# A second weight piece split ahead of the expert stage, its banks ordered by release, and new ranks for an instruction planner

## The chip, the core and the metric

The kernel runs on one core of a Trainium2 chip. The metric is the device time of one execution in microseconds, taken as the median of several runs. TensorE multiplies matrices into eight PSUM banks; VectorE (DVE), ScalarE (ACT) and GpSimd (POOL) do the work between the products; SyncE (SP) issues most of the loads and stores.

## The reference

Three layers follow each other, on 4 sequences of 576 tokens with 8 heads of 64:

```python
scores = scale * q @ k.T ; causal mask ; a = softmax(scores) ; local = a @ v
q_p = where(q > 0, q, exp(q) - 1) + 1
mem_out = (q_p @ M_prev) / (q_p @ z_prev + 1e-6)
x = sigmoid(beta) * mem_out + (1 - sigmoid(beta)) * local      # tokens 2304 x 512
logits = x @ w_gate ; e = argmax(logits) ; gate = softmax(logits)[e]
y[e tokens] = gate * (relu(x @ w1[e]) @ w2[e])                 # 8 experts, 512 -> 1024 -> 512
h = y @ w_in ; g = where(h > 0, h, exp(min(h, 0)) - 1)
out = g @ w_out                                                # 512 -> 2048 -> 512
```

## The kernel before

**Three stages.** Attention handles 16 pairs of heads (`pair(p)`, four pairs to a sequence). The expert stage (`moe`) handles tiles of 128 tokens of one expert (`mtile(t)`, NTM = 23 of them). The last layer is `moe2`. Each stage is a `phase`: its operations are declared with a cost and a priority, and `Plan.order` on the host lists them in time. At each step it takes the engine that can start earliest, and among the operations that could start within `slack` of that moment the one of lowest priority number. The instructions are issued engine by engine in the order of that list. So a priority decides only between operations that the plan holds for ready at nearly the same time, and a cost that is told wrongly moves instructions on every engine. The dictionary `KNOBS` holds the priorities (`off` per step of a pair; `m_x`, `m_1`, `m_h`, `m_fl` per kind of step of a tile), the engines that may take a step (`es`, `xe`, `wh`), and the slack of attention (`sa`) and of the expert stage (`sm`).

**A pair.** TensorE turns k and q (L92), makes five blocks of scores (L645, L649, L656), turns the exponentials back (L92), and multiplies them with v (L748). It then multiplies the result by the identity and the gate's weights (L538, `rw`), and VectorE reads that out, scaled (L777), and adds the memory part (L789; on GpSimd except in the last pair).

**The gate and routing.** After each sequence `gate_plan` picks the experts and writes a table (L824 to L903); after three of them `routing(early)` names the first NE = 4 tiles, whose weights are then loaded (`tile_weights`, L1120) and whose tokens are gathered. The fourth gate and the second routing (L936 to L1033) run inside the expert stage.

**A tile.** Products are made in three parts: high half by high half, low by high, high by low. So each of eight weight pieces of 128x1024 needs a cast to its high half (L1162 on DVE, L1159 on ACT in tile 0) and a subtraction for its low half (L1165, DVE only). Piece n = 2k + q lies in raw bank k. For tiles after the first the two steps stand behind a flag that skips them when the expert is the one of the tile before (`wsplit`, `fh` and `fl`, L1264 and L1269; two pieces to a step; the plan counts `m_if` for each). A tile's first product (L1288) uses pieces 0 to 3, its second (L1331) pieces 4 to 7; between them stand the ReLU (L1298), the transposes (L1313) and the split of the hidden values (L1159, L1165).

**The seam.** `first_parts` prepares tile 0 inside attention: it turns the gathered tokens (L1145), splits them (`x0`), and splits the pieces in `c.wq`, which is piece 0 alone, with the low priority `first`. These buffers lie in the pool `ep`, which outlives attention's pool `ap`. All other buffers of the expert stage lie in `mp`, which takes the place of `ap`. The expert stage has eight PSUM banks: four for the first product (`c.rg`), three for transposes, gate and routing (`c.rt`), one for the second product (`c.ry`). Attention uses the same memory as four tiles of two banks (`c.rx`).

Of the kernel before, what the change touches and what calls it, by code (L numbers as in the profile page):

```python
# [39 lines left out]
NS = 8  # L40
assert NE <= -(-((B - 1) * S - E * (P - 1)) // P)
# [53 lines left out]
class Plan:  # L95
# [140 lines left out]
    "xe": ("ACT", "DVE"), "he": ("ACT",), "re": [("ACT",), ("ACT", "DVE")], "m_ld": 3500.0, "m_x": -2208.9, "m_1": -1447.9, "m_h": -4434.5, "m_lag": 0.0,  # L236
    "m_if": 700.0, "m_fl": -3000.0, "m_wl": 300.0, "wa": 0, "wa0": 10022.449169040721, "wa1": 23927.854833523612, "wt": 1, "wp": 16, "wj": 2000.0,
# [3 lines left out]
    "nv": 2, "na": 2, "na4": 2, "nx": 2, "nls": 2, "wide": 1, "de": ("DVE", "POOL"), "busy": [0, 0, 0], "early": 120578.4, "late": 500, "mld": -2631.6,  # L241
    "gate": 345828.7, "warm": [52, 0.0, 200.0], "qe": ("DVE",),
    "off": {"tk": 898454.0, "tq": 882278.5, "hk": -760325.6, "hq": -759364.9, "px": 735151.8, "phi": 1087364.4, "S3": -529669.6, "S4": -1296033.8, "S2": -790035.1, "S1": -972813.3, "S0": -1302605.5, "min3": -50550.3, "min4": -410935.5, "min2": 719181.7, "min1": -45115.7, "min0": 332677.3, "exp3": 329358.7, "exp4": 631684.7, "exp2": -50550.0, "exp1": 518666.4, "exp0": 344677.0, "T3": 859665.0, "T4": 626578.9, "T2": 622423.5, "T1": 518666.8, "T0": 516520.2, "Te3": -47668.1, "Te4": 807182.8, "Te2": -1296012.9, "Te1": -509705.8, "Te0": -561958.2, "fin": -50955.8, "mm": 807201.2, "md": -1303158.8, "ms": 238704.4, "avA": -328031.8, "avB": -684654.8, "ave": -328185.5, "rw": -1410391.2, "ls": -829501.3, "add": -8135.8},
    "es": {"x": ("ACT",), "T0": ("ACT",), "T3": ("ACT",), "k": ("ACT", "DVE"), "T1": ("ACT", "DVE"), "T4": ("ACT", "DVE"), "q": ("ACT", "DVE"), "T2": ("ACT", "DVE")},
    "wait": 25, "first": 1087370.1, "stick": 1227967.1,
# [222 lines left out]
def cv(n):  # L468
    return 70 + 1.04 * n
# [705 lines left out]
def moe(tc, c, w1, w2, tiles):  # L1175
# [30 lines left out]
    def mtile(t):  # L1206
        pr = 1000.0 * t
        rw = t % 2 if t < NTM else 1
# [20 lines left out]
        if t:  # L1229
            pl.op("PE", 436, f, r=[sg], w=[wx], prio=pr + K["m_x"])  # L1230
        else:
            xh.index, xl.index = r_xh.free.pop(0)[1], r_xl.free.pop(0)[1]
        for _ in range(t > 0):
            split(c, lambda: wx.t, lambda: xh.t.rearrange("p c n -> p (c n)"), lambda: xl.t.rearrange("p c n -> p (c n)"), 512,
                  [wx], xh, xl, pr + K["m_x"], True, K["xe"], ("DVE",))

        flags = {}
        for e, eng in (("ACT", mybir.EngineType.Activation), ("DVE", mybir.EngineType.DVE)) if t else ():
            def mk(e, eng):
# [5 lines left out]
                pl.op(e, 450, f, r=[("sw", part)], w=[("flag", e, t)], prio=pr + K["m_fl"])  # L1245
            mk(e, eng)

        def wsplit(k, pr):
# [4 lines left out]
            if not t:  # L1253
                for q in range(2):
# [3 lines left out]
                    split(c, lambda q=q: src(q), lambda n=n: whi[n], lambda n=n: wlo[n], 1024, [("raw", rw, k)], keys[0][q], keys[1][q], pr, False, K["wh"][n], K["wl"][n])  # L1258
# [11 lines left out]
            pl.op("ACT", K["m_if"], fh, r=[("flag", "ACT", t), ("raw", rw, k)], w=keys[0], prio=pr)  # L1270
            pl.op("DVE", K["m_if"], fl, r=[("flag", "DVE", t), ("raw", rw, k)] + keys[0], w=keys[1], prio=pr)
# [4 lines left out]
        for cc in range(4):  # L1276
            def mk(cc):
                p1 = pr + K["m_1"] + 10 * cc
# [16 lines left out]
        for hf in range(2):  # L1295
            def mk(hf):
# [3 lines left out]
                def fv():  # L1300
# [3 lines left out]
                      prio=pr + K["m_h"])  # L1304
            mk(hf)
        hs = []
        for k in range(2):
            def mk(k):
                wt, hh, hl = Slot(rt), Slot(r_hh), Slot(r_hl)

                def f():
                    for j in range(4):
                        nc.tensor.transpose(wt.t[:, j * P:(j + 1) * P], sh.t[:, (4 * k + j) * P:(4 * k + j + 1) * P], c.ident)  # L1313
                pl.op("PE", 436, f, r=[(sh, k)], w=[wt], prio=pr + K["m_h"])
                split(c, lambda: wt.t, lambda: hh.t.rearrange("p c n -> p (c n)"), lambda: hl.t.rearrange("p c n -> p (c n)"), 512,
                      [wt], hh, hl, pr + K["m_h"], True, K["he"], ("DVE",))
# [4 lines left out]
        for q in range(4):  # L1321
            def mk(q):
# [11 lines left out]
                for jj in range(2):  # L1334
                    pl.op("PE", 3 * 216, mm(jj), r=[hh, hl, *wk], w=[y], prio=pr + 10 * q)
# [12 lines left out]
        pl.op(("ACT", "DVE"), (ca(512), cv(512)), (fa, fv), r=[y, sg], w=[sy], prio=pr + 500)  # L1348
# [248 lines left out]
def kernel(ctx, tc, q, k, v, M_prev, z_prev, beta, w_gate, w1, w2, w_in, w_out, out):  # L1597
# [43 lines left out]
    with ExitStack() as s1:  # L1641
# [3 lines left out]
        c.wq = [[ep.tile([P, 1024], F32R, name=f"wq{n}{i}") for i in range(2)] for n in range(1)]  # L1645
# [24 lines left out]
        with ExitStack() as s2:  # L1670
# [5 lines left out]
            banks, _ = psum(s2, "pm", 8)  # L1676
            c.rg, c.rt, c.ry = Ring("g", banks[:4]), Ring("t", banks[4:7]), Ring("y", banks[7:])
            
            def build():
# [3 lines left out]
                routing(tc, c, c.rt, False, c.K["late"])  # L1683
# [3 lines left out]
            phase(build, c.K["sm"])  # L1687
# [42 lines left out]
```

## Time and profile before

| what | value |
|---|---|
| median of 3 runs (lowest to highest) | 924.95 us (924.58 to 926.37) |
| the profiled execution | 925.45 us |
| its span from first to last instruction | 923.7 us |
| attention, to the first expert product | 0 to 213.4 us |
| TensorE busy | 894.0 us, 97% |
| VectorE, ScalarE, GpSimd busy | 66%, 48%, 13% |
| mean granted TensorE clock | 0.996 of full speed |

The profile is of one execution. Its rows give the start of an instruction or group from the start of the span, how long it was busy, and in brackets how long its engine had been idle before it and what ended that wait. Busy time of TensorE counts matmuls that overlap in its pipeline once. PE is TensorE multiplying, PEld its weight loads.

### The profile page before, as it was taken

What the parts mean: (1) busy time and instruction counts of PE and PEld (TensorE: products, weight loads), DVE (VectorE), ACT (ScalarE), POOL (GpSimd) and SP (SyncE); (2) the same over time, 40 slices, a digit from 0 to 9 for tenths busy, and PEclk for the clock granted to TensorE, in tenths of its full rate; (3) what the DMA queues carried; (4) which work ended last, traced back from release to release, by engine and by line L of the source; (5) the groups of instructions that cost most, each with busy time, mean ns of one, the idle gap of its engine ahead of it and who ended that gap; (6) DMA issues with size and microseconds to landing.
All of it is one profiled execution on the core that took longest, in us unless ns stands there. A gap on an engine that the chain in (4) does not pass through costs nothing. (4 is left out here: it accounts for less than half of the span.)

```text
span 923.7 us, 19288 instructions
## 1 busy us (share of the span) xinstructions
PE 894.0 (97%) x7404; PEld 739.9 (80%) x7404; DVE 611.6 (66%) x1105; ACT 444.0 (48%) x875; POOL 117.7 (13%) x176
## 2 busy tenths in 40 slices
PE   7999999998999999999999999999999999999995
PEld 4777777776788888888887889988888888888894
DVE  4778686987755687458996795555555566555553
ACT  5888888885543574458775642221222122122211
POOL 1111111122001222111211100010001000100100
PEclk9999999999999999999999999999999999999999
DMA  6334343456325985699983630010001010100000
GB/s 119 89 79 129 68 126 71 121 197 219 131 103 185 341 289 175 211 327 324 328 329 119 239 115 12 24 45 1 24 24 46 0 35 6 41 1 1 34 13 23
DMA packets 97111, 110.05 MB, mean 119 GB/s; under 512 B 65391, under 2 KB 65391, under 8 KB 94705
## 3 DMA queue, kind: packets, MB, share of 16 engines
q1 hardware_dynamic: 90992, 95.26, 32.4%
q0 software_dynamic: 4800, 13.18, 3.9%
q8 instruction: 59, 0.97, 0.4%
q10 hardware_dynamic: 1216, 0.30, 0.1%
q14 instruction: 44, 0.35, 0.1%
HBM read 87.94 MB, written 23.41 MB: 121 GB/s over the span
## 5 line engine op out<-in xcount | busy, mean ns | idle before, releaser
L1539 ACT ACTIVATE elu<-pt 128x512 f32<-128x512 f32 x72 | 43.1, 598 | 265.7 <-PE pt L1531 265.7
L1564 PE MATMUL pt<-w,gh 128*128 128x512 f32 x432 | 134.2, 392 | 0.5 <-DVE gh L1443 0.5
L1331 PE MATMUL pm<-w,hh 128*128 128x512 f32 x368 | 125.0, 401 | 0.8 <-ACT y L1344 0.8
L1547 DVE TENSOR_SCALAR elu<-elu 128x512 f32<-128x512 f32 x72 | 30.8, 428 | 126.8 <-ACT elu L1539 126.7
L1564 PEld LDWEIGHTS pt<-w,gh 128*128 128x128 f32 x432 | 79.6, 188 | 16.3 <-DVE gh L1443 0.9
L1564 PE MATMUL pt<-w,gl 128*128 128x512 f32 x216 | 84.2, 390 | 0.0
L672 ACT ACTIVATE a<-pat,st 128x128 f32<-128x128 f32 (+2 forms) x144 | 78.2, 548 | 8.1 <-DVE st L667 5.0
L1331 PEld LDWEIGHTS pm<-w,hh 128*128 128x128 f32 x368 | 69.2, 188 | 14.4 <-ACT y L1344 1.2
L667 DVE TENSOR_REDUCE st<-pat 128x2 f32<-128x256 f32 (+4 forms) x80 | 63.7, 798 | 18.8 <-PE pat L649 14.7
L1331 PE MATMUL pm<-w,hl 128*128 128x512 f32 x184 | 71.9, 391 | 0.3 <-DVE hl L1165 0.3
L1531 PE MATMUL pt<-yTh,w 128*128 128x256 f32 (+1 forms) x288 | 69.2, 319 | 0.0
L1551 DVE SCALAR_TENSOR_TENSOR tnh<-tnh,elu 128x512 f32<-128x512 f32 x72 | 49.6, 690 | 8.9 <-ACT tnh L1543 2.8
L1288 PE MATMUL pm<-w,x 128*128 128x512 f32 x216 | 51.9, 392 | 1.1 <-DVE w L1165 0.9
L1446 DVE TENSOR_TENSOR gl<-tnh,gh 128x512 fp32r<-128x512 f32 x72 | 49.6, 691 | 4.2
L1531 PEld LDWEIGHTS pt<-yTh,w 128*128 128x128 f32 x288 | 49.2, 190 | 3.9
L1555 DVE SCALAR_TENSOR_TENSOR tnh<-pt,tnh 128x512 f32<-128x512 f32 x72 | 49.6, 691 | 3.3
L645 PE MATMUL pat<-ab 64*128 64x128 f32 (+3 forms) x256 | 46.9, 474 | 2.1 <-ACT ab L595 2.1
L789 POOL TENSOR_TENSOR raw<-ms,ls 128x80 f32<-128x80 f32 (+2 forms) x45 | 30.2, 696 | 141.9 <-DVE ls L777 128.1
L1288 PEld LDWEIGHTS pm<-w,x 128*128 128x128 f32 x216 | 40.2, 188 | 10.1 <-DVE w L1165 1.4
L1165 DVE TENSOR_TENSOR hl<-pm,hh 128x512 fp32r<-128x512 f32 x46 | 31.5, 686 | 25.1 <-ACTq L1262 14.4
L1564 PEld LDWEIGHTS pt<-w,gl 128*128 128x128 f32 x216 | 40.5, 188 | 9.0 <-DVE gl L1446 0.4
L1531 PE MATMUL pt<-yTl,w 128*128 128x256 f32 (+1 forms) x144 | 45.9, 318 | 0.0
(336 smaller groups left out, 1982.3 us busy)
## 6 DMA issues: line engine op xcount, KB each, us to landing
wraw<-in_moe_w_dram SPq DMA_DIRECT2D x24, 1024.0 KB
wrbw<-in_moe_w_dram SPq DMA_DIRECT2D x12, 1024.0 KB
wide<-in_moe_w_in_dram SPq DMA_DIRECT2D x16, 512.0 KB
wf<-half SPq DMA_DIRECT2D x32, 256.0 KB
wide<-in_moe_w_out_dram SPq DMA_DIRECT2D x16, 512.0 KB
wide<-wf SPq DMA_DIRECT2D x9, 512.0 KB
v<-in_v_dram SPq DMA_DIRECT2D x32, 128.0 KB
wraw<-yd SPq DMA_DIRECT2D x14, 258.0 KB
```

Of the source, the lines that this page charges most:

```text
L645: nc.tensor.matmul(s.t[:, 512 * h:512 * h + n], row(1)[hs, i * P:(i + 1) * P], row(0)[hs, 0:n], start=True, stop=False)
L667: nc.vector.tensor_reduce(ss.t[:, 2 * i:2 * i + (2 if i < 4 else 1)], src(), axis=AX.X if i < 4 else AX.XY, op=ALU.min)
L672: nc.scalar.activation(sa[i].t[:, h, :] if i < 4 else sa[4].t[:, 0:S].rearrange("p (y n) -> p y n", y=2), src()[:, h, :] if i < 4 else src ...
L1165: nc.vector.tensor_sub(lo(), src(), hi().bitcast(F32))
L1288: nc.tensor.matmul(g[hf].t, a.t[:, cc, :], b[:, 512 * hf:512 * (hf + 1)], start=(cc == 0 and n == 0), stop=(cc == 3 and n == 2))
L1331: nc.tensor.matmul(y.t, a.t[:, 2 * (q % 2) + jj, :], b[:, 512 * jj:512 * (jj + 1)], start=(q == 0 and jj == 0 and n == 0), stop=(q == 3 an ...
L1446: nc.vector.tensor_sub(lo(), src(), hi().bitcast(F32))
L1531: nc.tensor.matmul(h.t[:, n * j + n0:n * j + n1], w(cc, a, ft), b(cc), start=(cc == 0 and x == 0), stop=(cc == 3 and x == 2))
L1539: nc.scalar.activation(se.t, h.t, AF.Exp)
L1551: nc.vector.scalar_tensor_tensor(st.t, st.t, 0.0, se.t, op0=ALU.min, op1=ALU.mult)
L1555: nc.vector.scalar_tensor_tensor(st.t, h.t, 0.0, st.t, op0=ALU.max, op1=ALU.add)
L1564: nc.tensor.matmul(acc[a].t, y.t[:, n * j + P * a:n * j + P * (a + 1)], wsub(1, k, ft // 2)[:, ft % 2, :], start=(ft == 0 and x == 0), sto ...
```

## The change

- `NWQ` = 2: `c.wq` holds pieces 0 and 1, so piece 1 too is split by `first_parts` within attention, and its two buffers move from `mp` to `ep`.
- The eight banks of the expert stage are dealt to the rings in the order in which the plan of attention frees its four double tiles.
- The plan of the expert stage gets start times for TensorE and VectorE (`begin`), load times for tiles 1 to 3 (`load`), and costs of the conditional splits of tiles 1 to 3 (`same`: ScalarE, VectorE).
- Each step of tiles 0 to 3 gets an offset of its own to its priority (`moff`, 84 numbers between -33046 and 32440), through `at`. The second routing gets its own priority `late2`, apart from the last gate's `late`.
- Nearly all numbers of `off`, and `hd`, `mem`, `early`, `gate`, `mld`, `first`, `stick`, are other ones; `sa` and `sm` are larger; in `es` the transposed weights T0 and T3 may now go to both engines, T1 and T2 go to ScalarE alone and T4 to VectorE alone.

```diff
+NWQ = 2
...
-    "xe": ("ACT", "DVE"), "he": ("ACT",), "re": [("ACT",), ("ACT", "DVE")], "m_ld": 3500.0, "m_x": -2208.9, "m_1": -1447.9, "m_h": -4434.5, "m_lag": 0.0,
+    "xe": ("ACT", "DVE"), "he": ("ACT",), "re": [("ACT",), ("ACT", "DVE")], "m_ld": 3500.0, "m_x": -10379.5, "m_1": -1436.3, "m_h": -11048.4,
-    "m_g": -500, "wq": 0.64, "sa": 70.4, "sm": 50.0, "s2": 0.0, "hd": 270570.9, "mem": -170390.9, "xg": 4,
+    "wj": 2000.0, "m_g": -500, "wq": 0.64, "sa": 79.1, "sm": 91.9, "s2": 0.0, "hd": -55445.7, "mem": 172588.0, "xg": 4,
...
-    "es": {"x": ("ACT",), "T0": ("ACT",), "T3": ("ACT",), "k": ("ACT", "DVE"), "T1": ("ACT", "DVE"), "T4": ("ACT", "DVE"), "q": ("ACT", "DVE"), "T2": ("ACT", "DVE")},
-    "wait": 25, "first": 1087370.1, "stick": 1227967.1,
+    "es": {"x": ("ACT",), "T0": ("ACT", "DVE"), "T3": ("ACT", "DVE"), "k": ("ACT", "DVE"), "T1": ("ACT",), "T4": ("DVE",), "q": ("ACT", "DVE"), "T2": ("ACT",)},
+    "begin": {"PE": 300.0, "DVE": 2100.0}, "load": {1: 100.0, 2: 5240.0, 3: 100.0}, "same": {1: (150.0, 150.0), 2: (1950.0, 2450.0), 3: (150.0, 150.0)},
...
+    "wait": 25, "first": 1063896.4, "stick": 1478029.9,
...
+        def at(x, y):
+            return pr + y + K["moff"].get(f"{x}{t}", 0.0)
...
-                tile_weights(tc, c, (w1, w2), t, j, prio=pr - 2900 + 900 * j, dma=5830 if t == 1 else K["m_ld"])
+                tile_weights(tc, c, (w1, w2), t, j, prio=pr - 2900 + 900 * j, dma=K["load"].get(t, K["m_ld"]))
...
-            pl.op("PE", 436, f, r=[sg], w=[wx], prio=pr + K["m_x"])
+            pl.op("PE", 436, f, r=[sg], w=[wx], prio=at("x", K["m_x"]))
...
-            pl.op("ACT", K["m_if"], fh, r=[("flag", "ACT", t), ("raw", rw, k)], w=keys[0], prio=pr)
-            pl.op("DVE", K["m_if"], fl, r=[("flag", "DVE", t), ("raw", rw, k)] + keys[0], w=keys[1], prio=pr)
+            ci = K["same"].get(t, (K["m_if"], K["m_if"]))
+            pl.op("ACT", ci[0], fh, r=[("flag", "ACT", t), ("raw", rw, k)], w=keys[0], prio=at(f"sh{k}t", pr - 1000.0 * t))
+            pl.op("DVE", ci[1], fl, r=[("flag", "DVE", t), ("raw", rw, k)] + keys[0], w=keys[1], prio=at(f"sl{k}t", pr - 1000.0 * t))
...
-        c.wq = [[ep.tile([P, 1024], F32R, name=f"wq{n}{i}") for i in range(2)] for n in range(1)]
+        c.wq = [[ep.tile([P, 1024], F32R, name=f"wq{n}{i}") for i in range(2)] for n in range(NWQ)]
...
             banks, _ = psum(s2, "pm", 8)
+            banks = [banks[2 * k + h] for _, k in sorted(c.rx.free) for h in range(2)]
             c.rg, c.rt, c.ry = Ring("g", banks[:4]), Ring("t", banks[4:7]), Ring("y", banks[7:])
...
-                routing(tc, c, c.rt, False, c.K["late"])
+                routing(tc, c, c.rt, False, c.K["late2"])
...
-            phase(build, c.K["sm"])
+            phase(build, c.K["sm"], **c.K["begin"])
```

The other steps of a tile take their priority through `at` in the same way.

## Rows read from the trace of the kernel before

**Rows 1.** The page: engines' busy us; then a group of expert products: busy us, mean ns.

```profile
PE 894.0 (97%) x7404; PEld 739.9 (80%) x7404; DVE 611.6 (66%) x1105; ACT 444.0 (48%) x875; POOL 117.7 (13%) x176
...
L1288 PE MATMUL pm<-w,x 128*128 128x512 f32 x216 | 51.9, 392 | 1.1 <-DVE w L1165 0.9
```

**Rows 2.** Windows by stage: length, then busy us of each engine, clock, DMA, GB/s.

```profile
0.00:205.00 205.00, 193.75 (x3765) 149.17 (x3765) 156.22 (x356) 166.56 (x435) 33.67 (x77) 0.99 0.44 113
205.00:245.00 40.00, 35.35 (x295) 27.59 (x294) 30.37 (x79) 22.08 (x36) 8.17 (x10) 1.00 0.55 195
```

**Rows 3.** Windows of the junction of the two stages, and one well inside the second.

```profile
220.70:226.00 5.30, 4.62 (x26) 3.49 (x26) 4.83 (x7) 3.01 (x6) 0.46 (x3) 1.00 1.00 380
248.00:260.00 12.00, 12.00 (x60) 10.12 (x60) 6.97 (x8) 7.65 (x11) 1.18 (x1) 1.00 0.21 67
```

**Rows 4.** Timeline of the junction: start, us, engine, instruction, count, idle before.

```profile
211.16 0.86 PE L538 MATMUL pat<-iw,xT 64*64 64x72 f32 x40
211.70 0.69 DVE L1165 TENSOR_TENSOR x<-pat,x 128x512 fp32r<-128x512 f32 x1
212.31 0.96 DVE L777 TENSOR_TENSOR ls<-pat,st 128x432 f32<-128x432 f32 x2
213.19 1.10 DVE L789 TENSOR_TENSOR raw<-ms,ls 128x48 f32<-128x48 f32 x4
213.42 1.63 PE L1288 MATMUL pm<-wq,x 128*128 128x512 f32 x6 [1.40 <-DVE raw L789]
214.33 1.30 DVE L1162 CAST w<-wraw 128x1024 fp32r<-128x1024 f32 x2
...
215.54 6.90 DVE L1165 TENSOR_TENSOR w<-wraw,w 128x1024 fp32r<-128x1024 f32 x6
216.81 3.94 PE L1288 MATMUL pm<-w,x 128*128 128x512 f32 x16 [0.95 <-DVE w L1165]
```

**Rows 5.** Timeline inside the expert stage: eighteen products in a row.

```profile
465.07 4.25 PE L1288 MATMUL pm<-w,x 128*128 128x512 f32 x18
```

**Rows 6.** TensorE's timeline: first score product of two plain pairs.

```profile
100.42 0.49 PE L645 MATMUL pat<-ab 64*128 64x128 f32 x4
112.07 0.49 PE L645 MATMUL pat<-ab 64*128 64x128 f32 x4
```

**Rows 7.** Waits of TensorE up to 213 us: total, times, longest.

```profile
PE pat L92 <- ACT aA L526: 2.3, 1, 2.3
PE pat L92 <- ACT a L672: 2.2, 6, 0.5
PE pat L645 <- ACT ab L595: 2.1, 3, 0.9
```

**Rows 8.** Timeline: splits and cover at the end of attention.

```profile
196.26 0.69 DVE L1162 CAST wq<-wraw 128x1024 fp32r<-128x1024 f32 x1
198.03 1.22 DVE L1165 TENSOR_TENSOR wq<-wraw,wq 128x1024 fp32r<-128x1024 f32 x1
...
211.15 0.17 DVE L755 SCALAR_TENSOR_TENSOR st<-pat,omg 128x10 f32<-128x10 f32 x1 [3.44 <-ACT xT L526]
```

**Rows 9.** Waits of SyncE's queue over the span: total, times, longest.

```profile
SPq L1120 <- DVE w L1165: 28.7, 3, 23.6
```

**Rows 10.** Timeline: the second gate's table beside GpSimd's additions.

```profile
182.43 1.70 POOL L789 TENSOR_TENSOR raw<-ms,ls 128x384 f32<-128x384 f32 x2 [4.61 <-DMA xd<-raw]
182.77 0.75 DVE L874 TENSOR_SCALAR raw<-col,grq 128x128 bf16<-128x128 f32 x1
184.14 0.27 DVE L874 TENSOR_SCALAR raw<-col,grq 128x128 bf16<-128x128 f32 x1
```

**Rows 11.** Timeline: tile 2's splits, the routing's comparison, and TensorE.

```profile
234.25 3.49 DVE L1269 TENSOR_TENSOR w<-wraw,w 128x1024 fp32r<-128x1024 f32 x3
238.84 0.15 DVE L949 TENSOR_TENSOR r_act<-r_act,r_early 72x2 bf16<-72x2 bf16 x1
239.04 0.16 PE L958 MATMUL pm<-r_act,triu 72*72 72x1 bf16 x1 [1.30 <-DVE r_act L949]
```

More of the change, by code (lines that the diff above doesn't have):

```diff
@@ L239 @@
+    "m_lag": 0.0, "m_if": 700.0, "m_fl": -7390.0, "m_wl": 300.0, "wa": 0, "wa0": 10022.449169040721, "wa1": 23927.854833523612, "wt": 1, "wp": 16,
+    "wj": 2000.0, "m_g": -500, "wq": 0.64, "sa": 79.1, "sm": 91.9, "s2": 0.0, "hd": -55445.7, "mem": 172588.0, "xg": 4,
     "wh": [("ACT", "DVE"), ("ACT", "DVE"), ("ACT", "DVE"), ("DVE",), ("ACT",), ("ACT", "DVE"), ("ACT", "DVE"), ("ACT", "DVE")],
     "wl": [("DVE",), ("DVE",), ("DVE",), ("DVE",), ("DVE",), ("DVE",), ("DVE",), ("DVE",)], "ord": [3, 4, 2, 1, 0], "rings": 4, "ab": 2, "nq": 2,
-    "nv": 2, "na": 2, "na4": 2, "nx": 2, "nls": 2, "wide": 1, "de": ("DVE", "POOL"), "busy": [0, 0, 0], "early": 120578.4, "late": 500, "mld": -2631.6,
@@ L244 @@
-    "es": {"x": ("ACT",), "T0": ("ACT",), "T3": ("ACT",), "k": ("ACT", "DVE"), "T1": ("ACT", "DVE"), "T4": ("ACT", "DVE"), "q": ("ACT", "DVE"), "T2": ("ACT", "DVE")},
-    "wait": 25, "first": 1087370.1, "stick": 1227967.1,
+    "nv": 2, "na": 2, "na4": 2, "nx": 2, "nls": 2, "wide": 1, "de": ("DVE", "POOL"), "busy": [0, 0, 0], "early": 227583.5, "late": 404.2,
+    "late2": -1146.3, "mld": -2420.5, "gate": 247809.4, "warm": [52, 0.0, 200.0], "qe": ("DVE",),
+    "off": {"tk": 1490122.7, "tq": 1134788.9, "hk": -629607.8, "hq": -485844.2, "px": 462606.7, "phi": 1134402.8, "S3": -313970.9, "S4": -1287369.8, "S2": -315915.3, "S1": -855187.7, "S0": -1603542.7, "min3": 910800.1, "min4": -858522.0, "min2": -53860.2, "min1": 685750.2, "min0": 29088.7, "exp3": 1066241.5, "exp4": -625354.6, "exp2": 681712.0, "exp1": 115280.8, "exp0": 1498211.0, "T3": 1035388.2, "T4": 596358.1, "T2": 528412.9, "T1": 425025.9, "T0": 318264.1, "Te3": 247142.8, "Te4": 246163.9, "Te2": -1603957.9, "Te1": 288963.7, "Te0": -619203.5, "fin": -865998.1, "mm": 26712.1, "md": -180887.2, "ms": 1120558.2, "avA": -90369.7, "avB": -485878.5, "ave": -643846.4, "rw": -1630474.1, "ls": -486744.1, "add": -319865.4},
@@ L1234, in mtile @@
             split(c, lambda: wx.t, lambda: xh.t.rearrange("p c n -> p (c n)"), lambda: xl.t.rearrange("p c n -> p (c n)"), 512,
-                  [wx], xh, xl, pr + K["m_x"], True, K["xe"], ("DVE",))
+                  [wx], xh, xl, at("xe", K["m_x"]), True, K["xe"], ("DVE",))
         flags = {}
@@ L1244, in f @@
                                               skip_runtime_bounds_check_because="made on the chip as a flag")
-                pl.op(e, 450, f, r=[("sw", part)], w=[("flag", e, t)], prio=pr + K["m_fl"])
+                pl.op(e, 450, f, r=[("sw", part)], w=[("flag", e, t)], prio=at("f" + e, K["m_fl"]))
             mk(e, eng)
@@ L1257, in wsplit @@
                         continue
-                    split(c, lambda q=q: src(q), lambda n=n: whi[n], lambda n=n: wlo[n], 1024, [("raw", rw, k)], keys[0][q], keys[1][q], pr, False, K["wh"][n], K["wl"][n])
+                    split(c, lambda q=q: src(q), lambda n=n: whi[n], lambda n=n: wlo[n], 1024, [("raw", rw, k)], keys[0][q], keys[1][q], at(f"w{n}t", pr - 1000.0 * t), False, K["wh"][n], K["wl"][n])
                 return
@@ L1277, in mk @@
             def mk(cc):
-                p1 = pr + K["m_1"] + 10 * cc
+                p1 = at("1t", K["m_1"] + 10 * cc)
                 if cc % 2 == 0:
@@ L1303, in mk @@
                 pl.op(es, [{"ACT": ca(512), "DVE": cv(512)}[x] for x in es], [{"ACT": fa, "DVE": fv}[x] for x in es], r=[g[hf]], w=[(sh, hf)],
-                      prio=pr + K["m_h"])
+                      prio=at(f"r{hf}t", K["m_h"]))
             mk(hf)
@@ L1334, in mk @@
                 for jj in range(2):
-                    pl.op("PE", 3 * 216, mm(jj), r=[hh, hl, *wk], w=[y], prio=pr + 10 * q)
+                    pl.op("PE", 3 * 216, mm(jj), r=[hh, hl, *wk], w=[y], prio=at("2t", 10 * q))
             mk(q)
@@ L1347, in fv @@
             nc.vector.tensor_scalar_mul(sy.t[:, 0:DM], y.t, sg.t[:, DM:DM + 1])
-        pl.op(("ACT", "DVE"), (ca(512), cv(512)), (fa, fv), r=[y, sg], w=[sy], prio=pr + 500)
+        pl.op(("ACT", "DVE"), (ca(512), cv(512)), (fa, fv), r=[y, sg], w=[sy], prio=at("yt", 500))
         if t < NE - NY:
```

8 lines of the change are left out of this document (3 added, 5 removed).

## The prediction

> **What bounds the kernel now.** I read the page first. TensorE is busy for 894.0 of 923.7 us, and no other engine passes 66% [rows 1]. So time can only come from stretches in which TensorE waits, or from work taken off TensorE, and the diff takes none off. Next come the windows by stage, to see where the missing 30 us lie. The first 205 us, nearly all of attention, leave 11.25 us idle, and the junction with the expert stage leaves 4.65 us in only 40 us [rows 2]. Well inside the expert stage a window of 12.00 us is busy for 12.00 us [rows 3], so there nothing can be gained.
>
> The timeline of the junction shows three losses. First, the last attention product ends at 212.02 us (211.16 plus 0.86), its result is read out by VectorE at L777 until 213.27 us, and the first expert product starts at 213.42 us after a wait of 1.40 us, although its token half was complete at 212.39 us (211.70 plus 0.69). Second, tile 0's 24 first products, issued as 6, 2 and 16, stop for the low half of weight piece 1: VectorE starts six such subtractions at 215.54 us, and the next 16 products begin at 216.81 us and end at 220.75 us [rows 4]. One such product is seen for 0.39 us [rows 1], and a dense run of 18 lasts 4.25 us [rows 5], so one follows the other by 0.227 us ((4.25 − 0.39)/17); 24 dense ones from 213.42 us would end at 219.03 us. The waits inside therefore cost 1.7 us. Third, 220.70 to 226.00 us is idle for 0.68 us [rows 3], and at 239.04 us TensorE ends a wait of 1.30 us for VectorE, told below.
>
> In attention, plain pairs follow each other at 11.65 us (100.42 to 112.07) [rows 6]. Waits on ScalarE up to 213 us come to 6.6 us: one of 2.3 near the start, six with 2.2 in all and three with 2.1 [rows 7].
>
> **The change part by part.** (a) The banks. Now the expert stage's first product gets banks in numeric order; the named releaser is VectorE at about 213.3 us, the end of the last read-out [rows 4]. After it, the first product's two banks come from the pair that the plan saw released first. Alone this gives at most the whole 1.40 us, and nothing if what holds the product is the addition at L789, which touches no bank.
>
> (b) Piece 1 split in attention. It adds one cast and one subtraction there, 0.69 and 1.22 us by piece 0's rows, so 1.91 us of VectorE, or 1.22 if ScalarE casts. No DMA is added: both pieces lie in one loaded bank, which was there at 196.26 us. The cover is VectorE's idle 3.44 us before 211.15 us [rows 8]. I cost it at nothing. If it lands ahead of the last read-out, the chain to 214.29 us slips by up to 1.22 us. It removes one subtraction of 1.15 us (6.90/6) from the junction [rows 4]. Tile 0's first raw bank also comes free earlier; a load on SyncE's queue waits up to 23.6 us for such a subtraction [rows 9], so tile 2's load can start earlier, and the stores queued behind it with it. TensorE shows no wait for that load now, so I add nothing.
>
> (a) and (b) don't add up. VectorE's last attention addition ends at 214.29 us and its first cast follows at 214.33 us, about 0.65 us each (1.30/2) [rows 4]. The next low half, piece 2's, is then ready at 214.98 + 1.22 = 216.2 us at the earliest, or 216.85 us behind two casts. After it ten products of pieces 2 and 3 remain: nine steps of 0.227 and 0.39 us bring the end to between 218.7 and 219.3 us, against 220.75 us. That is a gain of 1.45 to 2.05 us; I take 1.8. Bounds: 3.1 us if the two gains added fully, nothing if piece 2 merely takes piece 1's place behind more casts.
>
> One price for (b) is contention. VectorE's comparison took 0.75 us beside GpSimd's additions and 0.27 us after them [rows 10], so a split that falls on an addition may cost 0.5 us more. The Trainium skill's page SBUF — State Buffer, "Who interferes with whom", goes further: an instruction of VectorE with two inputs in SBUF is held up by a GpSimd instruction that reads SBUF. The subtraction is of that form, and the trace has none beside an addition. By that rule the sum would lose its cover and up to the 1.70 us of the two additions shown [rows 10].
>
> (c) Costs told to the planner. Tile 2's four subtraction steps were planned at 0.7 us each; the trace has 3.49 us for three subtractions alone, and a step has two, so 2.3 us [rows 11]. VectorE was thus later than planned, and TensorE stood 1.30 us in front of the routing product at L958, behind which all of tile 2's and tile 1's products queue, until the comparison at 238.84 us came through. The new entries are 1.95 and 2.45 us. I take 0.9 of the 1.30; bounds nothing and 1.30. The idle 0.68 us of 220.70 to 226.00 us may be filled by tile 1, whose weights the plan now expects to be the same expert's: I take 0.6; bounds nothing and 0.68. The separate ranks of the first tiles can undo either, which is the lower bound of both.
>
> (d) New ranks, engines and slack in attention. They change the order of the same instructions. The trace of before cannot show the new order. Bounds: a gain of 6.6 us, if every wait of [rows 7] went, and a loss of 15 pair steps at one such wait of 0.37 us (2.2/6), 5.5 us. I take nothing, since the plain pair is almost filled.
>
> **Sum.** The profiled execution took 925.45 us, 1.75 us more than its span. 925.45 − 1.8 − 0.9 − 0.6 = 922.15 us. It lies 0.5 us above the median of 924.95 us, so against the median the forecast is 921.6 us.
>
> Another reading makes the junction larger. Its weight loads fill 27.59 of 40.00 us, and 10.12 of 12.00 us in the dense window [rows 2, 3]. The Trainium skill's Perfetto Trace Analysis, "Identifying the Most-Contended Engine", holds that busy matmuls are a bad measure of headroom and that the share of weight loads is a good one. By that rule the junction has 40.0 − 27.59 × 12.00/10.12 = 7.3 us to give (an estimate) where the matmul rows show 4.65 us, and with all of it the sum would be 917.7 us against the median.
>
> **The rivals.**
> 1. Attention gains too. The waits of [rows 7] lie at irregular places, the start and the gates, which new ranks can move; against it, plain pairs have hardly any. Half of them gone gives 921.6 − 3.3 = 918.3 us.
> 2. No change in effect. The junction's end is set by VectorE's chain of read-out, additions and subtractions (213.19 to 222.44 us, almost without a gap) [rows 4]. If piece 1's split or new ranks delay that chain by what they save, all three terms vanish: 924.95 us.
> 3. Slower. The new order puts one wait of ScalarE's scores on every pair's path. Place: the weight transposes, which six times waited 0.37 us [rows 7]. Price: 15 × 0.37 = 5.5 us, so 921.6 + 5.5 = 927.1 us. It decides from 0.22 us a pair, where it eats the 3.3 us. Against it: plain pairs lack this wait today.
>
> **How the numbers follow.** A difference of 0.2%, 1.85 us, is about what a measurement of this kernel tells from none. The forecast has 0.50, rival 1 0.20, rival 2 0.16, rival 3 0.14. The forecast's own range is 919.5 to 924.0 us, by the bounds of (a) to (c). The range over all cases is 917.0 to 926.5 us: below it lies a small part of rival 1, above it about half of rival 3. Faster (below 923.1 us) takes 0.43 of the forecast's 0.50 and rival 1: 0.63. Same takes the rest of the forecast and rival 2: 0.23. Slower is rival 3: 0.14.
>
> **What would show it.** Right: a second split of the first piece in attention beside an unchanged pitch of 11.65 us; a wait before the first expert product below 0.4 us; tile 0's 24 products over within about 6.5 us; no wait above 0.5 us at L958. Wrong: a pitch that differs from 11.65 us by over 0.1 us, which 15 pairs multiply; attention's end later than now by over 1 us, for a late load or late split; or tile 0's products stopping at piece 2 as long as they now do at piece 1, with VectorE's additions at L789 still the releaser.

## The result and the profile after

The kernel after takes 939.07 us (median of 4 runs, 937.75 to 940.45) against 925.15 us for the kernel before beside it (4 runs, 924.58 to 926.37): a ratio of 1.0143, 95% interval 1.0127 to 1.0158. It is 13.9 us slower, where a gain of 3.3 us was forecast. The profiled execution took 939.33 us, its span is 937.4 us.

In the listing of after, a line of the attention part has a number higher by 4, one of the expert stage by 7 or 8: the token transposes, L1228 before, are L1235, the gathers L1138 instead of L1134, the read-out additions L793 instead of L789. In costs, exp_old, exp_new, no_off and no_costs the transposes are L1278 and the gathers L1181; in room the transposes are L1233.

I cut both spans at the same two events: the first expert product and the first product of the last layer's second matrix (L1564 before). The windows of after, and below them the second one of before (length; busy us of TensorE, its weight loads, VectorE, ScalarE, GpSimd; granted clock; DMA share; GB/s):

```profile
0.00:214.96 214.96, 199.72 (x3896) 154.80 (x3896) 164.42 (x374) 169.37 (x435) 37.42 (x79) 0.98 0.44 114
214.96:540.29 325.33, 309.07 (x1562) 256.77 (x1562) 222.00 (x349) 178.33 (x260) 59.26 (x69) 0.99 0.66 229
540.29:937.40 397.11, 388.30 (x1950) 329.83 (x1948) 227.64 (x394) 94.64 (x171) 20.39 (x29) 1.00 0.08 28
```

```profile
213.42:526.21 312.79, 305.15 (x1562) 255.50 (x1562) 223.10 (x347) 177.92 (x261) 61.13 (x68) 1.00 0.70 243
```

The three windows of before are 213.42, 312.79 and 397.49 us long. So attention lost 1.5 us, the expert stage 12.5 us, and the rest nothing. The stage has the same 1562 matmul records in both. TensorE's idle time in it rose from 7.64 to 16.26 us, by 8.6, and its busy time for the same work by 3.9 us. TensorE's waits from 213 to 540 us, after (total, times, longest; the longest groups):

```profile
PE pm L1235 <- DMA xg<-xd,r_tok: 9.9, 6, 3.4
PE pm L1235 <- DMA ex<-xd,r_tok: 2.7, 2, 2.4
PE pm L1296 <- DVE raw L793: 1.6, 1, 1.6
PE pm L1235 <- DVE half L1094: 1.2, 1, 1.2
...
```

Three of the four rows name one line, the transposes of a tile's gathered tokens, and they sum to 13.8 us; 12.6 of them are named as waits for a gather. Before had no wait there; its own waits in this stage are others, 7.2 us in all and none over 1.3. How such a wait comes about is seen by following one gather buffer, `ex`, through after's timeline:

```profile
295.94 0.69 ACT L1352 ACTIVATE y<-pm,ex 128x512 f32<-128x512 f32 x1 [2.17 <-PE pm L1339]
297.43 1.03 POOL L1381 DMA_INDIRECT yd<-y,r_pos  x1 [12.13 <-ACTq L1269]
298.77 1.03 POOL L1138 DMA_INDIRECT ex<-xd,r_tok  x1 [0.31 <-PE pm L1296]
306.00 0.74 PE L1235 MATMUL pm<-ident,ex 128*128 128x128 f32 x4 [2.40 <-DMA ex<-xd,r_tok]
...
326.10 1.20 POOL L1138 DMA_INDIRECT xg<-xd,r_tok  x1 [0.31 <-issue]
333.73 0.74 PE L1235 MATMUL pm<-ident,xg 128*128 128x128 f32 x4 [1.51 <-DMA xg<-xd,r_tok]
```

The read-out of a finished tile is the last reader of its gather buffer (it scales by the gate value, the buffer's last used column). Only then can GpSimd gather the tile that comes four later into it; here it starts at 298.77 us, and TensorE is at the transposes of that tile 7.2 us later, 2.40 us of which it stood still. The row at 297.43 us is GpSimd's scatter of the finished tile, which it issues ahead of the gather; in before it comes behind. It holds the gather back by 1.3 us. The same chain in before:

```profile
290.42 0.69 ACT L1344 ACTIVATE y<-pm,ex 128x512 f32<-128x512 f32 x1 [1.29 <-PE pm L1331]
291.38 1.02 POOL L1134 DMA_INDIRECT ex<-xd,r_tok  x1 [11.54 <-ACTq L1262]
307.95 0.63 PE L1228 MATMUL pm<-ident,ex 128*128 128x128 f32 x4
```

There 16.6 us lie between gather and transposes, and nothing waits. In the order of TensorE's instructions the transposes of tile 4 and later stand 24 products ahead of their own tile's first product before; after, those of tile 6 and later stand 51 to 66 ahead, so 27 to 42 products earlier, where a tile has 48. The gather did not move with them, since its buffer still comes free with the read-out. The code's planner counts 3.3 us for a gather (1040 + 650 + 734 + 900 ns); here it took over 7, in a stretch in which the DMA engines' busy share was 0.96 (298.77 to 306.00 us).

The clock adds to it. Windows of 10 us, after:

```profile
220.00:230.00 10.00, 5.55 (x24) 4.36 (x25) 3.12 (x4) 3.61 (x6) 1.13 (x3) 0.85 0.47 155
310.00:320.00 10.00, 10.00 (x51) 8.45 (x50) 4.23 (x9) 3.88 (x7) 2.50 (x3) 1.00 0.71 222
...
350.00:360.00 10.00, 10.00 (x44) 8.19 (x42) 7.37 (x10) 4.79 (x8) 2.32 (x3) 0.84 0.50 154
```

In the last window TensorE has work throughout but gets through 44 matmuls where it does 51 in the second: part of it ran at the lower level, 1.2 instead of 2.4 GHz, after the wait of 1.86 us at 348.82 us. The first and the last window lose at most 10 × (0.15 + 0.16) = 3.1 us, against the 3.9 us by which TensorE's busy time grew. The waits at the transposes, 13.8 us, stand against 8.6 us more of idle time, because some 5 us of before's own waits are gone.

Now attention. The start of the plain pairs:

```profile
40.13 0.49 PE L649 MATMUL pat<-ab 64*128 64x128 f32 x4
51.69 0.49 PE L649 MATMUL pat<-ab 64*128 64x128 f32 x4
63.26 0.49 PE L649 MATMUL pat<-ab 64*128 64x128 f32 x4
75.14 0.49 PE L649 MATMUL pat<-ab 64*128 64x128 f32 x4
```

The pitch is 11.56, 11.57 and 11.88 us, where [rows 6] gave 11.65: unchanged within a tenth, but for one pair. The waits that answer to [rows 7] are 3.5, 3.6 and 1.4 us, 8.5 in all instead of 6.6. The 1.5 us at the end of this stage is no more than a rough figure: six runs with before's order of attention (before, mx_early, exp_new, banks, room, costs) have the first expert product at 213.42 to 215.02 us, and six with after's (after, mx_back, x_lag, exp_old, no_off, no_costs) at 214.96 to 216.70; the means lie 1.8 us apart. The end of attention, after, answering to [rows 4, 8, 10]:

```profile
195.86 1.28 DVE L1166 CAST wq<-wraw 128x1024 fp32r<-128x1024 f32 x2
197.06 1.22 DVE L1169 TENSOR_TENSOR wq<-wraw,wq 128x1024 fp32r<-128x1024 f32 x1
...
203.67 2.99 POOL L793 TENSOR_TENSOR raw<-ms,ls 128x80 f32<-128x80 f32 x3 [10.82 <-DVE ls L781]
204.24 1.83 DVE L1169 TENSOR_TENSOR wq<-wraw,wq 128x1024 fp32r<-128x1024 f32 x1
205.99 1.27 DVE L626 SCALAR_TENSOR_TENSOR qpT<-ex,qpT 128x576 f32<-128x576 f32 x1
208.17 1.25 POOL L1138 DMA_INDIRECT ex<-xd,r_tok  x1 [1.51 <-DVE aB L533]
...
214.96 3.00 PE L1296 MATMUL pm<-wq,x 128*128 128x512 f32 x12 [1.58 <-DVE raw L793]
217.80 1.77 PE L1296 MATMUL pm<-w,x 128*128 128x512 f32 x6
```

Piece 1's subtraction did not fall into the idle 3.44 us of [rows 8]. It fell on GpSimd's additions, and the last pair's activation of q (L626) came behind it, at 205.99 us where before it ran at 197.35. TensorE then waits 1.2 us for it. The activation is also the last reader of `ex` in attention, so tile 0's gather into `ex` is later too (208.17 against 206.24 us). The row names another copy as what released the gather, but it starts 0.91 us after the activation's end, as in the run seam below (0.92 us), where the activation is named. The last two rows show the other side: twelve products in one run, and no stop for piece 1. And the 1.58 us in front of the first product stands as it did in [rows 4].

### The profile page after: what moved, and what is told of

Its sections match the earlier page's. It is cut to its first block, busy times and chain, and to the rows that moved or that the text cites. A ratio compares the mean times of both kernels' runs of the same rounds, so it can differ in the third digit from the quotient of the medians.

```text
span 937.4 us, 19284 instructions
## 1 busy us (share of the span) xinstructions
PE 897.1 (96%) x7404; PEld 741.4 (79%) x7404; DVE 614.1 (66%) x1115; ACT 442.3 (47%) x865; POOL 117.1 (12%) x176
## 5 line engine op out<-in xcount | busy, mean ns | idle before, releaser
L1339 PE MATMUL pm<-w,hh 128*128 128x512 f32 x368 | 130.1, 406 | 0.8 <-ACT y L1352 0.8
L793 POOL TENSOR_TENSOR raw<-ms,ls 128x80 f32<-128x80 f32 (+2 forms) x45 | 31.7, 728 | 140.8 <-DVE ls L781 126.7
L1306 ACT ACTIVATE h<-pm 128x512 f32<-128x512 f32 x46 | 27.3, 597 | 41.5 <-PE pm L1296 39.9
L1381 POOL DMA_INDIRECT yd<-y,r_pos x18 | 21.8, 1212 | 176.6 <-ACTq L1269 102.7
```

The source lines that it names most:

```text
L793: e.tensor_tensor(o, a, b, op=ALU.add)
L1339: nc.tensor.matmul(y.t, a.t[:, 2 * (q % 2) + jj, :], b[:, 512 * jj:512 * (jj + 1)], start=(q == 0 and jj == 0 and n == 0), stop=(q == 3 an ...
```

## The experiments

My theory was that the ranks of the expert stage, which the prediction had never priced, move the token transposes ahead of what their gathers can serve. The rival was that the attention part and the seam (the late activation, the late first gather) throw the stage out of step. No run leaves out work. In this table "first" is the start of the first expert product, "stage" the second window above, "5th" and "22nd" the start of the fifth and the twenty-second read-out of a tile, all in us of the profiled execution; the ratio is to the kernel before, run beside it.

| run | median us | ratio, 95% interval | first | stage | 5th | 22nd |
|---|---|---|---|---|---|---|
| before | 925.15 | | 213.42 | 312.79 | 290.4 | 501.3 |
| after | 939.07 | 1.0143 (1.0127 to 1.0158) | 214.96 | 325.33 | 295.9 | 516.1 |
| mx_early | 938.09 | 1.0128 (1.0095 to 1.0161) | 213.92 | 323.94 | 294.4 | 512.2 |
| mx_back | 941.15 | 1.0155 (1.0116 to 1.0195) | 216.06 | 325.04 | 304.9 | 517.0 |
| x_lag | 936.20 | 1.0103 (1.0071 to 1.0136) | 216.57 | 322.84 | 302.6 | 515.4 |
| seam | 930.04 | 1.0034 (1.0015 to 1.0052) | 216.51 | 316.03 | 295.6 | 508.3 |
| exp_old | 929.02 | 1.0027 (1.0007 to 1.0047) | 216.70 | 312.66 | 295.3 | 505.2 |
| exp_new | 956.50 | 1.0332 (1.0297 to 1.0368) | 215.02 | 343.07 | 300.6 | 534.1 |
| banks | 926.48 | 1.0004 (0.9991 to 1.0017) | 214.17 | 313.29 | 291.1 | 503.4 |
| seam_T4 | 926.84 | 1.0008 (0.9996 to 1.0020) | 214.67 | 313.78 | 291.9 | 504.1 |
| room | 926.15 | 1.0004 (0.9990 to 1.0019) | 214.64 | 314.42 | 292.4 | 503.3 |
| costs | 928.80 | 1.0039 (1.0022 to 1.0056) | 214.07 | 314.97 | 293.4 | 504.9 |
| no_off | 928.78 | 1.0024 (1.0004 to 1.0045) | 215.25 | 315.56 | 292.0 | 506.6 |
| no_costs | 933.53 | 1.0086 (1.0059 to 1.0113) | 216.54 | 318.03 | 299.8 | 510.4 |

The run banks has before's instructions in before's order; the 501.3 and 503.4 us in the last column show how far two executions of one order lie apart.

**mx_early: one rank alone.** The kernel before with

```
-    "m_x": -2208.9,
+    "m_x": -10379.5,
```

> The kernel before with one number changed: m_x -10379.5. Theory 1: the transposes move from 24 to about 66 products ahead of their tile's first product, waits behind gathers of 5 to 12 us appear in the expert stage: 931 to 938 us. Rival (the rank alone is harmless; only with the new slack and offsets it costs): 924.5 to 926 us.

938.09 us, at the upper end of the forecast: set alone, this one number costs as much as nearly the whole change. From tile 5 on the transposes stand 63 to 72 products ahead, TensorE waits 9.3 us behind gathers, and the chain is that of after, here with the buffer's read-out, the gather and the transposes:

```profile
319.11 0.69 ACT L1344 ACTIVATE y<-pm,xg 128x512 f32<-128x512 f32 x1 [2.08 <-PE pm L1331]
320.07 1.05 POOL L1134 DMA_INDIRECT xg<-xd,r_tok  x1 [9.69 <-ACTq L1262]
327.01 0.72 PE L1228 MATMUL pm<-ident,xg 128*128 128x128 f32 x4 [2.50 <-DMA xg<-xd,r_tok]
```

**mx_back and x_lag: two attempts to mend after.** In mx_back the same number goes back to −2208.9 in the kernel after; in x_lag it stays, and the planner is told that a tile's tokens are there 5.5 us later:

```
-            pl.op("PE", 436, f, r=[sg], w=[wx], prio=at("x", K["m_x"]))
+            pl.op("PE", 436, f, r=[sg], w=[wx], prio=at("x", K["m_x"]), lag=5500.0)
```

> The changed kernel with one number put back: the rank m_x of the token transposes and their splits, -2208.9 in place of -10379.5 (the offsets of tiles 1 to 3 stay). Theory 1 (the new rank puts a tile's token transposes so early in TensorE's order that the gather has not landed, and TensorE, which issues in order, stands): from tile 5 on they return to 24 products ahead of the tile's first product, the waits of 8.9 us behind gathers after 250 us vanish and with them the lower clock of 312 to 360 us, while the 4.9 us at tiles 1 to 3 stay: about 928 us (926 to 930). Rival (the wider slack or the other ranks cost the time, the transposes only stand where TensorE would wait anyway): 937 to 940 us.

> The changed kernel, all its numbers kept, but the planner holds the tokens of tiles 1 to 22 for landed 5.5 us later than it did (a lag on the step of the token transposes). Theory 1 in its narrower form (the rank does harm only because the plan believes gathers to land 3.3 us after their start, where they take up to 8.7): nearly all 13.8 us of waits vanish: 923 to 928 us. Rival (the early rank itself is the harm, whatever the plan believes of the gather): 933 us or more.

Neither time is what the theory forecast. But both runs mend the later tiles: from the fifth read-out to the twenty-second before takes 210.9 us, after 220.2, mx_back 212.1 and x_lag 212.8. In x_lag all the ranks of after are kept and the transposes of tile 6 and later stand 33 to 57 products ahead; only the planner's idea of the gather changed, and the waits behind gathers fell from 12.6 to 1.0 us. So in after, too, the waits behind gathers (7.4 us of them between those two read-outs) are most of what the later tiles lose.

What both lose lies in the first five tiles. From the first product to the fifth read-out before takes 77.0 us, after 81.0, mx_back 88.8 and x_lag 86.0. In x_lag this stretch has a granted clock of 0.94, and waits of 1.9 us for weights, 1.5 and 0.7 for the halves of x and up to 0.6 each for the flags, the hidden values and a read-out. So the rank is enough to cause the loss, but in after it is not alone; the first tiles have a cause of their own.

**exp_old and exp_new: cutting the change in two.** exp_old is after with all numbers that the expert stage reads set back; exp_new is after with the attention numbers and the one split piece of before.

```
exp_old: m_x, m_1, m_h, m_fl, sm, late as before; moff {}, begin {}, same {}, load {1: 5830}
exp_new: sa, hd, mem, early, mld, gate, off, es, first, stick as before; NWQ = 1
```

> The kernel after, with every number that the expert stage reads as it was before (m_x, m_1, m_h, m_fl, sm, the lateness of gate and routing, no offsets of tiles 0 to 3, one given cost for conditional splits and loads, no begin); the attention ranks, the second piece split in attention and the order of the banks stay. Theory 1 (the expert stage's new ranks cost the 12.5 us): the transposes stand 24 products ahead of their tile again, no wait behind a gather over 0.5 us after 240 us, the expert stage is back at 312 to 317 us, and what is left over the kernel before is what attention and the seam cost: 926 to 931 us. Theory 2 (the late seam, with its lower clock and late first gathers, throws the expert stage out of step): the stage stays at 320 us or more and the time at 934 to 940 us.

> The kernel after with the attention numbers of before and one piece split in attention, as before; the expert stage's numbers and the order of the banks are those of after. Theory 1: the expert stage alone carries the loss: gather waits of 8 us and more, stage at 322 us or more, 934 to 940 us. Theory 2: with attention and seam as before the expert stage keeps step, and the time is 924 to 929 us.

exp_old settles the theory against the rival: with the late seam still in it (first product at 216.70 us), its expert stage takes 312.66 us, as before. The 3.4 us by which it is over the kernel before beside it lie ahead of the first product (3.3 us in the profiled execution).

```profile
0.00:216.70 216.70, 200.98 (x3896) 155.31 (x3896) 164.72 (x374) 169.03 (x435) 37.24 (x79) 0.98 0.44 113
216.70:529.36 312.66, 306.54 (x1561) 257.00 (x1562) 223.25 (x349) 176.77 (x259) 60.47 (x68) 0.99 0.69 239
```

exp_new is far worse than either theory had it, 956.50 us. TensorE's waits in it from 300 to 510 us, and two windows early in its stage:

```profile
PE pm L1278 <- DMA xg<-xd,r_tok: 13.6, 7, 4.6
...
```

```profile
215.00:225.00 10.00, 5.30 (x20) 3.75 (x20) 6.68 (x9) 6.46 (x7) 3.85 (x7) 0.70 0.30 79
225.00:235.00 10.00, 9.12 (x29) 6.83 (x28) 7.32 (x20) 2.08 (x5) 0.00 (x0) 0.62 0.74 271
```

Its stage takes 343.07 us. It is the same wait, more often, with more of the lower clock. The place was right, the size not, and the parts don't add up: exp_old keeps 3.4 us of the loss, and exp_new, the other half, loses 31. The planner makes another order of the same numbers when one piece is split ahead than with two; why this one is so much worse was not followed.

**room: the same order, with room for the gathers.** If a transpose a tile earlier costs because its gather can't start, an earlier start must mend it. One more buffer was not tried; the buffer is released sooner instead. A small GpSimd copy takes the gate value out, and the read-out uses that; `m_x` is −3000 here, with which the transposes of tile 5 and later all stand 66 products ahead:

```
+        def fg():
+            nc.gpsimd.tensor_copy(sw.t, sg.t[:, DM:DM + 1])
+        pl.op("POOL", 100, fg, r=[sg], w=[sw], prio=pr + K["m_x"])
...
-            nc.scalar.activation(sy.t[:, 0:DM], y.t, AF.Copy, scale=sg.t[:, DM:DM + 1])
+            nc.scalar.activation(sy.t[:, 0:DM], y.t, AF.Copy, scale=sw.t)
```

> The kernel before with m_x at -3000, by which the token transposes stand 66 products ahead of their own tile's first product (in the run mx_early 63 to 72), and with the gate value copied out of the gathered tile by a small GpSimd copy, so that a gather buffer is free once its tile is transposed and the gather of four tiles later starts one to two tiles sooner. Theory 1, made sharper (an early transpose costs because its gather can't start before the tile that holds the buffer has been read out): no wait behind a gather over 0.5 us after 240 us, stage back at 312 to 315 us, 924 to 928 us. Rival (transposes that far ahead cost by themselves, through the banks and the halves of x that they hold, or through the contention of the gathers with the weight loads): 933 to 939 us as in mx_early.

926.15 us, the same as before within 0.2%, and no wait behind a gather, although the transposes stand 66 products ahead. The chain of `ex`, room:

```profile
299.80 0.63 PE L1233 MATMUL pm<-ident,ex 128*128 128x128 f32 x4
300.71 1.17 POOL L1134 DMA_INDIRECT ex<-xd,r_tok  x1 [5.74 <-PE pm L1233]
...
349.54 0.63 PE L1233 MATMUL pm<-ident,ex 128*128 128x128 f32 x4
```

The gather now starts as soon as the transposes have read the buffer and has 48.8 us until it is needed. With the transposes about where mx_early has them (66 products ahead, there 63 to 72) and the buffer released early, the loss of mx_early, some 11.5 us, does not come. The two runs differ in the value of `m_x` as well, −3000 against −10379.5, and −3000 without the copy was not run; what speaks for the release as the cause is the chain itself, and x_lag, where the same waits go with `m_x` as it is. The Trainium skill's Perfetto Trace Analysis, "Optimization Strategy", says that the same gap, repeated for a stretch on the engine that should be saturated, can mean that there is too little memory for the next tile, and names the count of buffers; the trace agrees, with 9.3 us of one repeated wait in mx_early and none in room, though here a sooner release did it and not one more buffer. Room is not faster than before, since before had no wait there to take.

**costs, no_off, no_costs: the first tiles.** costs is before with the accurate costs (its code is that of after, so it has the sorted banks too, which by the run banks change nothing); no_off and no_costs are mx_back without the offsets of tiles 0 to 3, and without the accurate costs.

```
costs:    begin {"PE": 300, "DVE": 2100}, load {1: 100, 2: 5240, 3: 100} and the same of after, added to before
no_off:   m_x -2208.9, moff {} in after
no_costs: m_x -2208.9, begin {}, same {}, load {1: 5830} in after
```

> The kernel before with the accurate costs alone (begin, load and same); all ranks, the piece and the banks as before. By the prediction's step (c): 1.5 us faster, 923 to 924 us. Rival: told that the load of tile 1 costs 100 ns, the planner sets the token transposes of tiles 1 to 3 after 18, 18 and 24 products instead of 24, 27 and 99, and TensorE stands behind their gathers: waits of 3 us and more between 217 and 235 us, a lower clock after them, 929 to 936 us.

> The kernel after with m_x back at -2208.9 (as in the run mx_back) and with no offsets of tiles 0 to 3; the accurate costs, m_1, m_h, m_fl and sm of after stay. If the singly ranked first tiles are what cost mx_back its 14 us before 305 us, the time is 927 to 931 us, as in the run exp_old. If the accurate costs are, 936 to 942 us.

> The kernel after with m_x back at -2208.9 and without the accurate costs (begin, load and same as in the code before); the offsets of tiles 0 to 3 stay. If the accurate costs are what cost mx_back its 14 us before 305 us, 927 to 931 us; if the offsets are, 936 to 942 us.

Told that tile 1's load costs 100 ns, the planner of costs sets the transposes of tiles 1 to 3 after 18, 18 and 24 products, where before has 24, 27 and 99:

```profile
219.87 0.63 PE L1278 MATMUL pm<-ident,xg 128*128 128x128 f32 x4
224.08 1.13 PE L1278 MATMUL pm<-ident,xg 128*128 128x128 f32 x4 [3.58 <-DMA xg<-xd,r_tok]
```

The wait of 1.30 us in front of the routing product [rows 11] is gone, as meant, and a longer one has come. The time, 928.80 us, lies between the forecast and its rival. As for mx_back's first five tiles: its 88.8 us from the first product to the fifth read-out become 76.8 without the offsets, as in before, and 83.3 without the accurate costs. So the offsets are needed for the whole of that loss, and the costs make it larger by 5.5 us. With `m_x` and the offsets both set back, no_off is 2.7 us over the kernel before beside it, of the 13.9 us. Which single offset does it was not tried, nor after with its offsets alone set back.

**seam, seam_T4, banks: steps (a) and (b) by themselves.** seam is before with two split pieces and the sorted banks; banks has the banks alone; in seam_T4 the split of piece 1 is also held back until the last pair's last transposed scores are read out:

```
seam and seam_T4:
-        c.wq = [[ep.tile([P, 1024], F32R, name=f"wq{n}{i}") for i in range(2)] for n in range(1)]
+        c.wq = [[ep.tile([P, 1024], F32R, name=f"wq{n}{i}") for i in range(2)] for n in range(2)]
seam, seam_T4 and banks:
+            banks = [banks[2 * k + h] for _, k in sorted(c.rx.free) for h in range(2)]
seam_T4, in attention and in what the split of a piece reads:
-        c.se = se
+        c.se, c.xlast = se, (sB, 4)
...
-[("raw", 0, 0)]
+[("raw", 0, 0)] + ([c.xlast] if q else [])
```

> The kernel before with two parts of the change: piece 1 split in attention as well, and the expert stage's banks dealt in order of release; all ranks as before. By the prediction's terms (a) and (b): a gain of 1.8 us, 923.3 us (922 to 924.5), the wait before the first expert product below 0.4 us. Rival (that wait does not hang on which bank is taken, and the split lands on GpSimd's additions): 924.5 to 927 us with the wait still above 1 us.

> The kernel before with the order of the banks alone. The order of instructions and of waits is that of before on all engines; the first products write into another pair of banks. By the prediction's step (a) up to 1.4 us before the first product go: 923.2 to 924.6 us, and that wait is under 0.4 us. By the rival (the product waits for the addition behind the read-out of the last product of attention, not for the bank) nothing changes: the wait stays at 1.3 to 1.6 us and the time within 0.2% of the kernel before.

> The kernel before with the second piece split in attention and the order of the banks, but the split of the second piece held until the last pair's last transposed scores are read out, so that the last pair's activation of q stays where it was and the split falls into VectorE's idle time before the first tile's. If the run seam lost its 3 us because that activation, and with it the first tile's gather, came 11 us later, this one has the gather back at 206 to 207 us, the first product at 213 to 214 us and a time of 922.5 to 925 us (1 us of split is taken off the stretch after 212 us). If instead a second split beside GpSimd's additions is what costs, or the pieces split in attention have no use, it is 926 to 930 us.

banks changes nothing: the wait for the addition stands, 1.40 us, though the banks under the product are others. In it the read-out (L777) ends at 214.02 us, the first addition (L789) at 214.14, and the product starts at 214.17, 0.03 us behind the addition. Behind other instructions of VectorE it starts 0.05 to 0.06 us later (the routing product of [rows 11], the first product in seam), so the times speak for the addition:

```profile
213.06 0.96 DVE L777 TENSOR_TENSOR ls<-pat,st 128x432 f32<-128x432 f32 x2
213.94 1.11 DVE L789 TENSOR_TENSOR raw<-ms,ls 128x48 f32<-128x48 f32 x4
```

In seam the activation of q is at 208.67 us, and the gather that waits for it shows it:

```profile
205.32 1.83 DVE L1165 TENSOR_TENSOR wq<-wraw,wq 128x1024 fp32r<-128x1024 f32 x1
208.67 0.74 DVE L622 SCALAR_TENSOR_TENSOR qpT<-ex,qpT 128x576 f32<-128x576 f32 x1
210.33 1.25 POOL L1134 DMA_INDIRECT ex<-xd,r_tok  x1 [2.59 <-DVE qpT L622]
...
216.51 4.60 PE L1288 MATMUL pm<-wq,x 128*128 128x512 f32 x12 [1.72 <-DVE x L1165]
```

The first product then waits for its tokens (`x`) and no longer for an addition, and the time, 930.04 us, is above both forecasts.

In seam_T4 the activation is back in its place, and piece 1's split lies in the idle time that the prediction had named as its cover:

```profile
198.63 0.76 DVE L622 SCALAR_TENSOR_TENSOR qpT<-ex,qpT 128x576 f32<-128x576 f32 x1 [0.41 <-ACT qpT L612]
...
207.52 1.24 POOL L1134 DMA_INDIRECT ex<-xd,r_tok  x1 [0.16 <-issue]
208.90 0.69 DVE L1162 CAST wq<-wraw 128x1024 fp32r<-128x1024 f32 x1
209.62 1.23 DVE L1165 TENSOR_TENSOR wq<-wraw,wq 128x1024 fp32r<-128x1024 f32 x1
...
214.67 3.01 PE L1288 MATMUL pm<-wq,x 128*128 128x512 f32 x12 [1.40 <-DVE raw L789]
217.52 3.15 PE L1288 MATMUL pm<-w,x 128*128 128x512 f32 x12
```

The loss of seam is gone (926.84 us, ratio 1.0008), though the time is above the 922.5 to 925 us forecast. So the place of the split was its cause. Holding the split back moved it off GpSimd's additions and the activation back to its place at once; that it was the late activation is read from seam's wait for `x`, not shown apart. Tile 0's 24 products take 6.0 us (214.67 to 220.67) instead of 7.3, so the split of piece 1 does give 1.3 us there. It isn't seen in the time: at the fourth gate's table and the second routing TensorE then waits 2.2 us (0.33, 1.54 and 0.32, between 243.5 and 247.0 us), which before did not have; before's 1.30 us at the routing product is gone instead.

## Why the prediction was wrong

**The step that failed** is the first part's sentence that well inside the expert stage "nothing can be gained", by a window of 12.00 us busy for 12.00 us [rows 3]. The reading of the window was right, and the use of it wrong: a full stage has no wait to give back, but a new order can put waits into it. The diff gives that stage new ranks (m_x, m_h, sm and others), and no term, bound or rival of the prediction stands for them; the lowest it allowed the new ranks to do was to undo step (c)'s own gain. In the profiled executions the stage lost 12.5 us with them and nothing with the old ones (exp_old, 312.66 us), and m_x alone, put into before, costs it 11 (mx_early). The rows that would have told were in the trace: the gather at 291.38 us that starts after the read-out at 290.42, and the transposes at 307.95. The 16.6 us between them is the room that there is. A tile's 48 products take 12.3 us, so transposes 27 to 42 products earlier leave 5.8 to 9.7 us of it (an estimate), and a gather here takes over 7.

**Step (a), the banks.** The upper bound was taken into the 1.8 us, and the lower one held: nothing. That condition was in the prediction, and its own row names the addition, `raw L789`, as the releaser, where the prediction read the last read-out. The run banks shows that the bank does not matter.

**Step (b), piece 1.** The gain at the junction was sized rightly (1.3 us of products, in seam_T4). "Costed at nothing" failed, because the order put the split where the cover was not, and moved the activation of q behind it: the first product came at 216.51 us in seam, against 213.42 to 215.02 us in the runs with before's order. The price of contention, put at 0.5 us from [rows 10], measured 0.61 for the subtraction (1.83 against 1.22) and 0.99 for the three additions (2.99 against 2.00). The Trainium skill's SBUF — State Buffer, "Who interferes with whom", says that an instruction of VectorE with two inputs in SBUF contends with a GpSimd instruction that reads SBUF. The trace agrees: both are longer where they overlap, and in seam_T4, where they don't, they take 1.23 and 2.01 us. Each got longer by half.

**Step (c), the accurate costs.** 1.5 us gained were forecast; alone they lose 2.75 us (928.80 against 926.05 beside it). The wait of [rows 11] was read rightly, and it goes, but what is late next was not asked: the transposes of tiles 1 to 3, 3.58 us behind a gather.

**Step (d), attention.** Nothing was taken, and nothing came: the pitch is the same, and the last pair's first score product is at 198.50 us against 198.90. Rival 3 was on the right side by luck: the loss that it named, on every pair, is not there. The reading by the share of weight loads (the Trainium skill's Perfetto Trace Analysis, "Identifying the Most-Contended Engine") gave the junction 7.3 us to give back. No run here shows such a gain: from the first product to the fifth read-out, which holds most of the junction, before takes 77.0 us and the shortest run 76.8 (no_off).

**The range.** The bounds given for (a) to (c) add up to a gain of nothing to 5.1 us, which is 919.9 to 924.95 us and not 919.5 to 924.0; nothing hangs on it, the measured time lies far outside either.

**What stays open.** That the first product waits for an addition, which writes no operand of it, is only read from the times and the named releaser, and why it should is not known. Nor was it tried which offset costs mx_back its first tiles, and why exp_new's order is 17 us worse than after's. No version tried is faster than before.

## What to carry over

A stage in which the busiest engine hardly waits gives a new order nothing to win, but the order can lose there on every tile; price a new rank in such a stage by the slack between the transfer that feeds the step and the step, and ask what lets that transfer start. Moving a consumer earlier is worth nothing while its producer is held by a buffer: release the buffer first, or leave the consumer. And a planner told better costs makes another order, whose waits are at other places than the one that the costs were to mend.

## What was not expected of the hardware

A gather of one tile, from the start of its instruction to the end of TensorE's wait for it, took between 3.4 and 8.7 us in after. At the first tiles it was 3.44 us (216.80 to 220.24, DMA share 0.36), 3.70 us (218.12 to 221.82, share 0.72) and 7.87 us (219.47 to 227.34, share 0.63). Later it was 7.23 us (298.77 to 306.00, share 0.96), 7.63 us (326.10 to 333.73, share 1.00) and 8.67 us (340.15 to 348.82, share 0.93). So the longest came beside full DMA engines, but the share alone does not tell the time. The clock did not fall after each such wait: after 2.40 us at 306.00 it stayed at 1.00, after 1.86 us at 348.82, which followed 1.51 us at 333.73, the next window had 0.84. In mx_early the windows from 220 and from 325 us hold waits of 2.02 and 2.50 us; one shows 0.83, the other 1.00:

```profile
220.00:230.00 10.00, 7.61 (x36) 5.84 (x35) 8.86 (x21) 3.78 (x7) 1.66 (x3) 0.83 0.96 365
...
325.00:335.00 10.00, 7.99 (x41) 6.84 (x42) 6.71 (x10) 4.96 (x8) 0.00 (x0) 1.00 0.86 329
```

So a wait's price was its length in one place, and in another up to 1.7 us more, 10 × (1 − 0.83).
